# A new fixed order of all events in a delta-rule attention with a feed-forward layer

## The chip, the cores and the metric

One core of a Trainium2 chip runs the whole kernel in one launch. The metric is the device time of one execution in microseconds (us). The core has five engines that run their own instruction streams and wait for each other by semaphores: TensorE (PE, matrix products; PEld is its weight load), VectorE (DVE), ScalarE (ACT), GpSimd (POOL) and SyncE (SP), which here issues all transfers (DMA).

## The reference

What is computed, cut to what matters:

```python
# q, k, v: (4, 8, 768, 48), beta: (4, 8, 768), float32
k_n = k / (norm(k, axis=-1) + 1e-06)
state = zeros((B, H, D, D))
for t in range(S):
    y[:, :, t] = einsum('bhd,bhde->bhe', q[:, :, t], state)
    v_old = einsum('bhde,bhd->bhe', state, k_n[:, :, t])
    state = state + beta_t * einsum('bhd,bhe->bhde', k_n[:, :, t], v[:, :, t] - v_old)
x = y.transpose(0, 2, 1, 3).reshape(3072, 384)
h = x @ w_in                                   # w_in (384, 2048), float64
sp = maximum(h, 0) + log1p(exp(-abs(h)))
out = (h * erf(sp)) @ w_out                    # w_out (2048, 384), float64
```

## The kernel before, in words

The attention is cut into 12 chunks c of 64 time steps, with the 32 pairs of batch and head side by side. Per chunk: the squares of k (norm_sq, ACT L196), their sums (norm_sum, DVE L204), the norms and the factors gn and ga in 18 small steps (norm_ops, DVE L215 to L228), the products of k with itself (gram_mm, PE L255) and their scaling to the matrix A (gram_a, DVE L265). Two chunks make a group sg. A goes to DRAM (to_dram, L290) and comes back in 32x32 blocks (to_blocks, L299, tile gb). A triangular solve with 31 rows (solve_row, L316 a product, L318 an addition) inverts these blocks in tile xb; DVE does the first solve, POOL the other five. The result goes through DRAM again (put_blocks L323, from_blocks and from_blocks2 L330 and L338), is transposed (merge_t, DVE L345), and put together on PE (merge_e L353, merge_z L366, merge_m L379). Then the chain, 48 steps j (4 batches for each chunk): put_v (POOL L401, z from v and the norms), chain_u (PE L414, DVE L420), chain_s (L427), chain_y (L441), chain_m.

The outputs y are the rows x of the feed-forward layer, in 12 groups of 16 blocks: ffn1 (L631, nine products of fp16 halves), softplus and erf (ACT L653 and L658, DVE L662 and L671, ACT L669, POOL L675), ffn2 (L686 to L688), all with high and low fp16 parts. Both weights come as 24 raw pieces of 512 KB (tiles raw_in0 to 11 and raw_out0 to 11: w_load, SP L486) and pass a conversion to fp32: w_mask (ACT L493), w_sign (DVE L497), w_bits (DVE L502), w_sum (ACT L507, a copy of the absolute values that gives the maximum). The raw tiles share buffers with other tiles, so a load may wait for the w_sum of an earlier piece. When all 12 pieces of w_in are through: w_max, w_all, w_scale (DVE L511, PE L476, DVE L519), the scaled identity w_idsc (L549), the high parts w_hi (ACT L541) and the low parts (w_lo1, PE L557 and L558; w_lo2, ACT). x needs a scale as well (x_max L577, x_scale L584, x_lo L619).

At the start ACT clears xm and z by copies of a zero tile (clear_x, L164 and L166); POOL clears qp and xb. PE runs 15 zero products (warm, L153) and 270 more, one by one as events (fill), which only keep it busy.

All these steps are events with a time from a planner's formulas. The list is sorted by that time, and then put in another order by a tuple of 2554 numbers, ORDER (line 33 of the file): each engine executes its instructions in that order. This tuple alone decides what stands behind what on an engine:

```python
ev.sort(key=lambda e: (e[0], e[1]))
if ORDER:
    ev = [ev[i] for i in ORDER]
with tc.manual_schedule(engines={E.PE, E.Activation, E.DVE, E.Pool, E.SP}):
    for _, _, fn in ev:
        fn()
```

ACT loads a table of functions (table, L138) wherever the next event needs another one than the last.

## Time and profile before

| what | value |
|---|---|
| runs | 660.6, 660.2, 662.53 us (median 660.6) |
| profiled execution | 664.21 us |
| its span | 662.4 us, so 1.8 us lie around it |
| granted clock of PE, mean | 0.98 |
| busy, share of the span | PE 97%, PEld 75%, ACT 74%, DVE 63%, POOL 47% |
| zero products on PE (L153) | 285, 52.6 us |
| table loads on ACT (L138) | 147, 188.6 us |

A row of a timeline gives the start, the length, the engine, the line, the operation, out<-in with shapes, how many alike in a row (x2), and in brackets how long the engine sat idle before it and what ended that. A row of a window gives the stretch and its length, the busy time of each engine in the order PE, PEld, DVE, ACT, POOL with the number of instructions, then the granted clock, DMA's share and GB/s. L12 is line 12 of the kernel. One execution stands behind the profile; its own time is 3.6 us above the median of the runs.

### The profile page before, as it was taken

To read this page: it belongs to the slowest core of one execution; us is meant where nothing else is said; L and a number is where in the kernel's file an instruction comes from. 1 tells how busy PE (TensorE), PEld (TensorE's weight loads), DVE (VectorE), ACT (ScalarE), POOL (GpSimd) and SP (SyncE) were. 2 spreads that over 40 slices of the span, in tenths; PEclk is the share of its full clock that TensorE was granted. 3 is DMA by queue.
4 is the path that set the end of the run, shared out by engine and by line. 5 is a ranking of instruction groups with operands and counts; after the bars stand their busy time and mean duration, and the time that the engine had idled before them with its cause. 6 is when DMAs were issued, how large, how long until landed. Compare 5 with 4: busy or idle time off the path is not lost.

```text
span 662.4 us, 21898 instructions
## 1 busy us (share of the span) xinstructions
PE 639.5 (97%) x9353; PEld 493.6 (75%) x9353; DVE 415.7 (63%) x976; ACT 491.2 (74%) x731; POOL 309.5 (47%) x492
## 2 busy tenths in 40 slices
PE   7978899899999999999999999999999999999996
PEld 5655586677788878778877788887787888777763
DVE  4986877976565966677766766767454666344230
ACT  6423369899988788978678567878768879698870
POOL 2000238837588708984169274424981412403130
PEclk9979769999999999999999999999999999999999
DMA  9879763035423371423527034123014201010110
GB/s 297 250 226 280 180 160 84 30 84 106 81 68 80 90 158 38 116 48 81 119 70 174 7 99 108 32 51 74 14 25 100 64 9 44 2 25 13 25 25 24
DMA packets 87395, 59.03 MB, mean 89 GB/s; under 512 B 67777, under 2 KB 77121, under 8 KB 87297
## 3 DMA queue, kind: packets, MB, share of 16 engines
q1 hardware_dynamic: 87296, 57.63, 35.2%
q8 instruction: 73, 1.20, 0.8%
q14 instruction: 26, 0.20, 0.1%
HBM read 43.45 MB, written 14.16 MB: 87 GB/s over the span
## 4 chain that ended last, share of the span: by engine, by line
PE 73%; DVE 10%; ACT 7%; DMA 4%; POOL 2%; issue 2%; SPq 1%; DVEq 0%; POOLq 0%; ACTq 0%
PE ph L631 24%; PE pr L686 9%; PE pr L687 8%; PE pr L688 8%; PE pc L441 3%; PE pc L414 3%; DMA raw_out<-w_out 3%; PE pm L379 3%; PE pg L255 2%; PE pq L255 2%; PE pc L427 2%; PE pz L366 2%; ACT L138 2%; PE pe L353 2%; ACT w_out L541 1%
## 5 line engine op out<-in xcount | busy, mean ns | idle before, releaser
L631 PE MATMUL ph<-xh,w_in 128*128 128x256 f16 x1152 | 206.7, 273 | 0.0
L138 ACT ACT_TABLE_LOAD x147 | 188.6, 1283 | 3.3 <-PEq L959 0.7
L631 PEld LDWEIGHTS <-w_in 128*128 128x128 f16 x1728 | 166.1, 98 | 28.1 <-issue 0.9
L631 PE MATMUL ph<-xl,w_in 128*128 128x256 f16 x576 | 157.1, 273 | 0.0
L675 POOL TENSOR_TENSOR H<-L,H 128x512 f16<-128x512 f32 x58 | 69.5, 1209 | 175.6 <-DVE H L671 122.9
L662 DVE SCALAR_TENSOR_TENSOR L<-ph,L 128x512 f32<-128x512 f32 x96 | 65.8, 688 | 102.2 <-ACT L L658 93.9
L686 PE MATMUL pr<-w_out,H 128*128 128x384 f16 x384 | 125.6, 327 | 0.0
L687 PE MATMUL pr<-w_out,H 128*128 128x384 f16 x384 | 125.3, 326 | 0.2 <-DVE w_out L568 0.2
L688 PE MATMUL pr<-w_out,H 128*128 128x384 f16 x384 | 125.3, 326 | 0.0
L401 POOL TENSOR_TENSOR z<-v,nm 64x192 f32<-64x192 f32 x96 | 53.2, 555 | 132.7 <-DMA v<-vtok 111.0
L653 ACT ACTIVATE L<-ph,xct 128x512 f32<-128x512 f32 x96 | 65.9, 687 | 58.3 <-PE ph L631 51.2
L318 POOL TENSOR_TENSOR xb<-xb,tmptmpg 128x31 f32<-128x31 f32 (+15 forms) x155 | 86.6, 559 | 12.1
L316 POOL TENSOR_TENSOR tmptmpg<-gb,xb 128x31 f32<-128x31 f32 (+15 forms) x155 | 80.7, 521 | 13.0 <-DMA be<-btok 3.2
L658 ACT ACTIVATE L<-L 128x512 f32<-128x512 f32 x96 | 59.3, 628 | 0.9
L688 PEld LDWEIGHTS <-H 128*128 128x128 f16 x384 | 37.5, 98 | 25.2 <-issue 0.4
L153 PE MATMUL warm<-zero 128*128 128x384 f16 x285 | 52.6, 347 | 1.1 <-DVE zero L144 1.1
L686 PEld LDWEIGHTS <-H 128*128 128x128 f16 x384 | 37.5, 98 | 20.7
L420 DVE TENSOR_TENSOR z<-pc,ga 64x192 f32<-64x192 f32 x88 | 31.2, 354 | 34.1 <-PE pc L414 32.2
L687 PEld LDWEIGHTS <-H 128*128 128x128 f16 x384 | 37.6, 98 | 19.8
L153 PEld LDWEIGHTS <-zero 128*128 128x128 f16 x285 | 28.7, 103 | 21.9 <-issue 4.7
L255 PE MATMUL pg<-kpg 48*64 48x64 f32 x736 | 28.0, 230 | 8.3 <-DVE qp L276 4.7
L669 ACT CAST H<-L 128x512 f16<-128x512 f32 x56 | 33.5, 609 | 2.5 <-DVE L L662 2.2
(139 smaller groups left out, 929.1 us busy)
## 6 DMA issues: line engine op xcount, KB each, us to landing
raw_in<-w_in SPq DMA_DIRECT2D x12, 512.0 KB, 5.8
raw_out<-w_out SPq DMA_DIRECT2D x12, 512.0 KB, 8.7
d<-A SPq DMA_DIRECT2D x22, 256.0 KB, 3.3
kpg<-kT SPq DMA_DIRECT2D x24, 192.0 KB, 4.7
k<-ktok SPq DMA_DIRECT2D x12, 384.0 KB, 4.2
qp<-qT SPq DMA_DIRECT2D x24, 192.0 KB, 3.9
v<-vtok SPq DMA_DIRECT2D x48, 96.0 KB, 2.8
out<-ob SPq DMA_DIRECT2D x48, 96.0 KB, 2.3
```

The lines of the kernel that those rows point to most:

```text
L138: se.add_instruction(mybir.InstLoadActFuncSet(name=nc.get_next_instruction_name(), act_func_set_id=i, ins=[], outs=[]))
L153: te.matmul(wp[0], zero[:, :P], zero, start=True, stop=True)
L316: eng.tensor_tensor(tv, G[:, s, s + 1:].unsqueeze(1).broadcast_to([P, ncol, nr]), Xv[:, :, s:s + 1].broadcast_to([P, ncol, nr]), op=ALU.mult)
L318: eng.tensor_tensor(Xv[:, :, s + 1:], Xv[:, :, s + 1:], tv, op=ALU.add)
L631: te.matmul(ph, w[:, i, kt * P:kt * P + P], G[x][:, :, ksl], start=(m == 0), stop=(m == 8))
L653: se.activation(unit(g, u), G["ph", u], AF.Softplus, bias=0.0, scale=G["ct"])
L658: se.activation(Lu, Lu, AF.Erf, bias=0.0, scale=1.0)
L662: ve.scalar_tensor_tensor(Lu, fg[g]["ph", u], HSC, Lu, op0=ALU.mult, op1=ALU.mult)
L675: (ve if u % (2 if g < GLE else GLM) == 0 else ge).tensor_tensor(G["gl", u], unit(g, u), G["gh", u], op=ALU.subtract)
L686: te.matmul(G["po"][a], gh[:, o, asl], wout_h[:, i, :], start=(i == 0), stop=False)
L687: te.matmul(G["po"][a], gh[:, o, asl], wout_l[:, i, :], start=False, stop=False)
L688: te.matmul(G["po"][a], gl[:, o, asl], wout_h[:, i, :], start=False, stop=(i == NFF - 1))
```

## The change

Nothing but the tuple ORDER differs. Its first numbers, before and after:

```diff
-ORDER = (0,1,2,12,7,21,22,24,25,28,30,34,36,37,40,42,44,45,49,51,33,27,3,5,6,98,4,244,143,8,251,100,17, ...
+ORDER = (1,2,409,374,53,49,191,95,197,137,401,415,238,5,108,45,173,432,373,269,3,222,437,213,257,64,279, ...
```

The same events in another order make nearly the same instructions: the same products, transfers and vector operations; ACT loads a table 142 times in place of 147, one of them in front of the first square (line L196). The order differs over the whole list, most in the opening.

The first place is DVE in the first solve. tmpT0_n is the product of row n, w_in_100 and w_out_101 are the tiles of the converted weights. Before, a part of the solve with its pieces:

```order
L316 TENSOR_TENSOR tmpT0_5_384<-gb0_333,xb0_135 128x156
L318 TENSOR_TENSOR xb0_135<-xb0_135,tmpT0_5_384 128x6x26
L497 TENSOR_SCALAR raw_in5_364<-raw_in5_364 128x512
L316 TENSOR_TENSOR tmpT0_6_388<-gb0_333,xb0_135 128x175
L318 TENSOR_TENSOR xb0_135<-xb0_135,tmpT0_6_388 128x7x25
L497 TENSOR_SCALAR raw_in0_391<-raw_in0_391 128x512
L316 TENSOR_TENSOR tmpT0_7_557<-gb0_333,xb0_135 128x192
L318 TENSOR_TENSOR xb0_135<-xb0_135,tmpT0_7_557 128x8x24
L497 TENSOR_SCALAR raw_out3_393<-raw_out3_393 128x512
```

Now the same rows, and the place where the first piece stands:

```order
L316 TENSOR_TENSOR tmpT0_5_530<-gb0_414,xb0_379 128x156
L318 TENSOR_TENSOR xb0_379<-xb0_379,tmpT0_5_530 128x6x26
L316 TENSOR_TENSOR tmpT0_6_533<-gb0_414,xb0_379 128x175
L318 TENSOR_TENSOR xb0_379<-xb0_379,tmpT0_6_533 128x7x25
L316 TENSOR_TENSOR tmpT0_7_536<-gb0_414,xb0_379 128x192
L318 TENSOR_TENSOR xb0_379<-xb0_379,tmpT0_7_536 128x8x24
```

```order
L316 TENSOR_TENSOR tmpT0_14_558<-gb0_414,xb0_379 128x255
L318 TENSOR_TENSOR xb0_379<-xb0_379,tmpT0_14_558 128x15x17
L497 TENSOR_SCALAR raw_out1_442<-raw_out1_442 128x512
L316 TENSOR_TENSOR tmpT0_15_576<-gb0_414,xb0_379 128x256
L318 TENSOR_TENSOR xb0_379<-xb0_379,tmpT0_15_576 128x16x16
```

Rows 0 to 14 have no piece between them any more. In the whole solve there were 11 w_sign and 5 w_bits (raw_in5, in0, out3, out1, in7 first); now there are 6 w_sign (out1, out3, in9, out10, in5, in6), 3 w_bits (out10, out1, out3) and the negative identity (L546). Ahead of the solve stand seven of each before and now; the rest moved behind it.

The second place is ACT at the very start. Before:

```order
L138 ACT_TABLE_LOAD
L164 CAST xm0_0_90<-zero_102 128x1024
L164 CAST xm0_1_91<-zero_102 128x1024
L164 CAST xm1_0_92<-zero_102 128x1024
L164 CAST xm1_1_93<-zero_102 128x1024
L166 CAST z0_94<-zero_102 128x384
L166 CAST z1_95<-zero_102 128x384
```

Now:

```order
L196 ACT_TABLE_LOAD
L196 ACTIVATE sq0_172<-k0_170 128x768
L196 ACTIVATE sq1_177<-k1_145 128x768
L164 CAST xm0_0_90<-zero_102 128x1024
L164 CAST xm0_1_91<-zero_102 128x1024
L164 CAST xm1_0_92<-zero_102 128x1024
L164 CAST xm1_1_93<-zero_102 128x1024
```

The squares of chunks 0 and 1 moved ahead of the ten copies of zeros; the squares of chunks 2 and 3 stand behind them, as all four did. On DVE the sums of squares 2 and 3 now stand between the norms and the factor gn0 of the first group.

The third place is the queue of SP around the end of the first solve (d2 is the result in DRAM, A2_0 and w_out_101 blocks of A from DRAM, xm the blocks of the result). Before:

```order
L486 DMA raw_out6_758<-w_out 128x1024
L394 DMA v2_774<-vtok 128x192
L245 DMA kpq2_780<-kT 48x1024 x2
L486 DMA raw_out4_790<-w_out 128x1024
L323 DMA d2_0_792<-xb0_135 64x1024
L323 DMA d2_1_796<-xb0_135 64x1024
L330 DMA w_out_101<-d1_1_323 32x16x32 x2
L394 DMA v1_891<-vtok 128x192
L338 DMA xm0_0_90<-d2_0_792 32x16x32
```

Now:

```order
L245 DMA kpg3_763<-kT 48x1024 x2
L486 DMA raw_in11_775<-w_in 128x1024
L486 DMA raw_out6_794<-w_out 128x1024
L323 DMA d2_0_796<-xb0_379 64x1024
L330 DMA A2_0_798<-d1_0_403 32x16x32 x2
L394 DMA v0_835<-vtok 128x192
L323 DMA d2_1_840<-xb0_379 64x1024
L338 DMA xm0_0_90<-d2_0_796 32x16x32
L338 DMA xm0_1_91<-d2_0_796 32x16x32
```

The loads of raw_out4 and raw_out5 moved behind the solve's way through DRAM, two small transfers now stand between the two halves of the result, and w_out's block transfer went ahead to the first round trip. At the start of this queue k1 and k0 are now first, where kpg0 was; kpg0 is sixth.

Elsewhere: the 270 zero products, in 8 runs before (14, 133, 7, 21, 69, 18, 5, 3), stand in 21 runs (55, 1, 3, 103, 12, 5, 2, 33, 15 and twelve of 1 to 9), all ahead of the first ffn1 as before. On POOL the put_v steps 7 and 9 moved ahead of the second solve's first row, and put_v(6) behind its row 7. In the middle of the list chain steps, merges and ffn groups changed places: between the last row of POOL's last solve (sg 5) and its first merge (chunk 10) stood twelve ffn groups, and now stand five, with more chain steps.

More of the change, by code (lines that the diff above doesn't have):

```diff
@@ new lines @@
+ORDER = (1,2,409,374,53,49,191,95,197,137,401,415,238,5,108,45,173,432,373,269,3,222,437,213,257,64,279,355,112,97,225,202,169,58,4,17,18,149,19,358,20,6,26,31,307,336,247,104,35,38,399,264,420,61,27,294,390,281,98,229,304,80,255,331,43,444,129,143,7,433,153,348,100,101,8,106,235,182,338,103,47,206,155,33,164,408,178,193,46,312,21,72,76,83,60,354,146,501,521,148,15,267,528,410,162,379,421,25,389,351,286,244,11,292,234,260,317,157,302,295,428,132,12,446,87,13,387,429,251,533,549,41,440,280,330,344,175,357,123,48,135,81,366,92,337,316,78,160,99,334,52,159,102,134,67,188,385,119,89,183,284,158,296,56,242,324,272,340,270,187,210,384,425,320,118,199,113,165,107,125,342,42,32,184,16,323,150,339,392,411,84,383,190,192,195,413,328,39,365,127,171,117,419,189,62,154,82,246,258,311,211,218,70,378,91,293,376,249,196,314,181,221,347,30,224,65,219,259,86,131,233,240,248,256,262,268,276,285,291,300,308,322,315,305,74,231,28,398,198,382,289,306,217,109,168,124,326,236,1301,369,205,71,327,121,431,156,290,111,36,142,274,287,489,261,176,161,447,418,352,241,152,377,88,367,394,204,436,757,93,9,303,282,350,333,141,479,319,203,341,349,435,208,215,298,506,473,512,275,301,449,170,40,130,73,207,356,517,14,416,363,313,239,179,535,68,370,375,273,201,404,174,10,122,140,51,24,310,57,69,318,50,381,386,361,391,216,362,332,212,180,237,400,359,396,63,299,230,343,288,405,402,209,128,214,407,422,412,417,452,423,232,329,110,194,393,23,29,22,151,335,450,474,480,514,85,228,223,252,271,406,79,424,263,126,442,309,55,66,243,77,475,120,345,522,75,427,755,441,138,266,200,434,380,430,486,453,438,115,177,360,34,226,388,54,44,325,116,186,483,166,526,534,136,90,283,94,403,459,114,364,297,145,172,462,245,448,139,461,460,265,468,353,470,439,144,481,372,516,414,471,464,133,463,485,482,346,467,503,488,537,642,609,466,395,37,484,59,167,487,371,472,147,477,507,495,465,497,476,253,491,632,524,527,494,518,445,492,163,532,493,508,496,443,523,455,511,531,96,451,541,278,185,540,538,490,454,456,499,469,551,785,498,818,580,866,513,457,546,458,545,636,519,502,500,515,554,505,530,520,561,550,644,547,662,510,536,525,552,504,321,666,560,105,478,509,555,564,559,567,574,575,589,569,553,625,576,583,562,586,558,581,250,594,597,565,557,590,660,277,587,670,601,602,604,572,611,615,624,578,614,593,227,598,220,397,529,791,577,608,618,620,426,588,626,368,568,634,596,683,543,765,542,254,585,629,556,591,539,592,548,792,633,649,616,647,631,621,595,599,652,637,655,795,796,657,798,603,606,639,573,544,600,610,659,679,635,579,640,566,645,563,584,664,671,605,800,776,607,623,643,682,690,692,685,794,613,630,687,571,693,706,646,674,648,570,612,678,651,680,582,686,619,694,638,672,691,699,676,710,698,705,716,681,726,696,654,622,627,628,684,688,728,807,731,656,689,661,658,701,653,709,663,733,713,717,667,764,870,720,702,704,707,736,695,708,697,723,737,772,801,641,738,814,668,802,805,711,806,703,752,673,808,847,700,712,675,729,714,756,735,665,715,812,819,775,718,782,821,742,677,778,747,841,848,719,779,751,769,777,788,721,783,797,740,780,781,784,722,826,836,758,744,988,761,724,725,766,852,827,787,786,669,771,820,773,803,910,727,774,743,730,835,748,789,804,732,859,811,824,825,790,902,842,861,734,793,885,879,829,851,739,810,854,822,833,809,741,745,860,823,869,813,878,746,749,817,750,945,864,895,816,830,828,839,753,754,799,880,832,907,1022,831,990,867,858,617,837,872,877,838,862,871,882,853,874,834,759,857,843,887,845,849,855,840,650,916,760,929,850,873,856,922,1068,888,904,863,762,876,881,892,901,905,884,912,921,906,931,926,865,890,909,889,908,868,911,914,919,886,936,935,939,915,942,763,875,932,893,899,937,946,767,898,883,913,943,930,920,1111,897,947,844,894,925,933,1033,973,957,918,952,891,846,768,903,770,924,989,896,917,966,975,1035,934,938,951,950,962,961,941,1001,959,992,1004,995,1009,958,900,998,1279,1002,964,977,1011,963,983,1010,1053,1003,953,1012,968,1016,1034,981,1047,967,940,948,956,960,969,982,980,954,986,997,1021,971,994,1018,1000,1036,1173,1023,1052,1015,1040,1024,1037,1041,1008,991,1054,979,923,1007,1013,1058,1062,955,1116,984,993,1005,1014,1020,996,944,1064,949,927,928,1057,1061,1199,999,1006,1134,1185,1123,1192,0,1118,1066,1194,1127,1027,970,1017,1209,1028,1029,1213,1025,1032,1051,1049,1042,1043,1128,965,1131,1138,1071,1038,1141,1044,1060,976,1210,1142,1139,1031,1087,1162,987,1065,1046,1059,1083,1086,1045,978,1144,1110,1048,1055,1026,1050,1067,1056,1063,1074,1082,1075,1204,1113,1088,1146,985,1099,1085,1106,1168,1175,1147,1156,1070,1077,1232,1093,1039,1069,1019,1098,1073,815,1079,1072,1239,1096,1109,1121,1030,1129,1158,1176,1178,1182,1180,1102,1219,1076,1080,1112,1126,1186,1094,1119,1133,1078,1104,1084,1103,1140,1270,1091,1090,1148,1089,1151,1248,1097,1152,1108,1184,1115,1100,1105,1117,1092,1313,1132,1201,1159,1136,1135,1143,1150,1164,1095,1122,1149,1206,1120,1124,972,1217,1225,1172,1177,1187,1154,1189,1114,1157,1207,1238,1153,1101,1188,1107,1125,1130,1137,1145,1190,1155,1163,1227,1245,1249,1174,1160,1167,1161,1241,1171,1179,1254,1214,1263,1216,1181,1191,1381,1183,1195,1170,1246,1251,1285,1327,1373,1196,1193,1264,1265,1291,1302,1289,1284,1200,1286,1234,1306,1414,1198,1269,1255,1197,1205,1240,1299,1242,1423,1211,1215,1267,1308,1314,1229,1226,1305,1247,1262,1212,1271,1250,1257,1253,1273,1203,1208,1272,1220,1275,1223,1231,1277,1230,1237,1309,1233,1202,1350,1338,1342,1280,1228,1236,1281,1292,1244,1260,1268,1274,1282,1295,1324,1288,1341,1434,1278,1319,1332,1312,1336,1165,1235,1326,1328,1290,1330,1218,1329,1335,1222,1400,1221,1346,1360,1304,1365,1243,1375,1340,1256,1287,1224,1347,1266,1293,1389,1343,1331,1321,1334,1345,1355,1390,1349,1294,1586,1166,1169,1356,1358,1457,1276,1252,1392,1351,1303,1399,1311,1551,1310,1362,1259,1283,1348,1354,1377,1383,1387,1396,1298,1406,1408,1296,1391,1378,1384,1339,1398,1407,1333,1418,1440,1394,1344,1409,1393,1395,1425,1364,1432,1447,1419,1307,1258,1436,1261,1426,1442,1451,1413,1369,1315,1412,1359,1361,1363,1422,1367,1372,1424,1370,1430,1438,1415,1374,1371,1382,1617,1441,1366,1325,1435,1443,1453,1376,1385,1471,1337,1473,1479,1488,1428,1466,1497,1297,1460,1468,1300,1316,1352,1318,974,1491,1421,1397,1386,1402,1427,1403,1450,1357,1411,1404,1469,1323,1322,1461,1521,1416,1433,1472,1437,1525,1579,1465,1353,1464,1476,1439,1530,1539,1540,1493,1455,1417,1511,1429,1452,1480,1474,1490,1475,1484,1478,1456,1379,1499,1458,1462,1081,1485,1556,1508,1510,1368,1560,1380,1388,1401,1496,1482,1503,1512,1517,1449,1317,1515,1514,1518,1523,1524,1548,1553,1594,1446,1448,1531,1459,1467,1410,1519,1527,1481,1445,1420,1431,1444,1489,1554,1674,1561,1529,1320,1533,1494,1495,1563,1504,1454,1564,1405,1572,1546,1646,1463,1522,1558,1507,1506,1574,1565,1626,1477,1487,1498,1632,1636,1697,1528,1595,1581,1660,1470,1513,1526,1648,1587,1569,1589,1562,1532,1541,1545,1573,1483,1492,1538,1578,1486,1720,1543,1680,1571,1655,1597,1592,1557,1609,1596,1576,1535,1600,1547,1593,1580,1620,1601,1610,1624,1661,1625,1634,1598,1614,1612,1672,1640,1582,1702,1544,1638,1552,1559,1568,1649,1722,1770,1618,1652,1685,1639,1611,1536,1616,1631,1653,1659,1689,1633,1602,1566,1650,1657,1585,1604,1570,1744,1605,1666,1804,1516,1622,1588,1619,1679,1627,1658,1577,1584,1591,1607,1500,1509,1520,1534,1542,1656,1549,1688,1501,1550,1673,1555,1567,1675,1575,1628,1635,1583,1703,1705,1683,1537,1706,1690,1692,1693,1677,1728,1637,1676,1641,1707,1682,1694,1712,1724,1730,1734,1590,1740,1603,1813,1708,1710,1714,1717,1718,1844,1613,1623,1630,1643,1751,1687,1695,1654,1738,1608,1615,1761,1621,1629,1642,1651,1668,1698,1741,1736,1739,1758,1755,1662,1763,1665,1599,1502,1505,1669,1742,1670,1789,1760,1798,1606,1764,1800,1743,1759,1780,1681,1696,1786,1709,1725,1746,1731,1664,1747,1933,1745,1667,1898,1819,1762,1823,1713,1723,1767,1754,1765,2073,1753,1756,1645,1700,1671,1729,1818,1732,1701,1704,1837,1820,1779,1840,1846,1802,1805,1809,1686,1843,1771,1691,1807,1815,1783,1816,1822,1684,1699,1772,1825,1826,1835,1748,1766,1773,1838,1715,2220,1782,1781,1868,1716,1711,1964,1777,1797,1647,1872,1721,1790,1799,1808,1644,1851,1811,1719,1727,1864,1803,1812,1784,1785,1829,1726,1866,1821,1788,1879,1793,1827,1737,1787,1794,1769,1855,1735,1857,1828,1926,1878,1832,1859,1871,1862,1904,1750,1913,1752,1861,1874,1865,1870,1858,1749,1757,1877,1768,1778,1795,1886,1836,1893,1663,1876,1775,1880,1850,1932,1888,1903,1678,1911,1883,1919,1907,1791,1842,1853,1935,1841,1830,1854,1948,1957,1940,1945,1869,1905,1942,1921,1875,1959,1909,1792,1801,1920,1887,1978,1980,1884,1988,1733,1774,1776,1939,1966,1796,1892,1974,1806,1975,1925,1890,1894,1923,1961,1833,1979,1927,1983,2058,1946,1982,1984,1997,1941,1958,2000,1912,1985,1994,1998,1956,1943,1963,1929,1973,1895,1814,1824,1834,1845,1860,1965,1873,2028,2032,1885,1891,1899,1906,1917,1969,1881,1900,2004,2085,2005,1901,1924,1908,1896,1810,1817,1953,2036,2045,1931,1910,1831,1938,1967,2015,2017,1971,2054,2059,2019,2021,1839,2031,2048,1972,2061,2003,1847,2020,2067,1856,2064,1992,1949,1990,2063,2066,1981,2069,1954,1962,2018,2052,1968,1867,1849,1928,1882,1889,1934,2010,2025,1897,1902,1936,2101,2130,2023,2030,1915,1986,1944,1947,1987,2171,2202,2037,1976,2158,1914,1952,1995,2040,2001,2070,2092,1989,1996,2122,1993,2002,1922,2078,2029,2009,2106,2026,2081,2034,2047,2099,2012,2024,2050,2013,1930,2039,2046,2053,2113,2055,2060,2051,2071,1937,1848,1951,2103,2014,2088,2038,2095,2056,2135,2100,2105,2033,1852,2035,2065,1960,1970,2207,2108,2097,2079,2087,1955,2109,2094,2116,1916,2104,2107,1918,2124,2043,2044,2118,2131,2132,2120,2139,2093,2068,2154,2083,1950,2138,2102,2231,2041,2117,2080,2151,2115,2084,2134,2136,1977,2159,1991,2086,2168,2123,2126,2112,2140,2314,2072,2114,2089,2170,2157,2125,2128,2164,2121,2129,1999,2006,2141,2149,2152,2180,2172,2174,2016,2027,2176,2173,2178,2076,2077,2183,2185,2042,2074,2184,2212,2190,2187,2137,2110,2188,2244,2049,2196,2198,2142,2144,2192,2008,2143,2211,2057,2062,2177,2204,2189,2182,2208,2075,2082,2090,2011,2191,2150,2155,2209,2091,2156,2214,2219,2147,1863,2148,2163,2237,2265,2249,2096,2218,2181,2166,2245,2225,2186,2098,2256,2215,2111,2213,2217,2194,2200,2167,2243,2227,2242,2216,2226,2230,2197,2251,2259,2201,2246,2233,2261,2258,2277,2007,2203,2205,2223,2279,2119,2127,2133,2248,2238,2240,2146,2278,2263,2229,2282,2287,2247,2195,2297,2348,2221,2267,2232,2274,2266,2368,2302,2234,2273,2311,2145,2153,2250,2268,2284,2292,2160,2275,2281,2169,2272,2269,2301,2313,2179,2294,2260,2271,2300,2252,2295,2280,2323,2326,2264,2285,2286,2288,2193,2315,2199,2327,2316,2332,2317,2318,2320,2283,2255,2206,2331,2162,2022,2325,2345,2339,2210,2340,2349,2222,2350,2293,2299,2334,2298,2306,2236,2165,2352,2224,2354,2355,2357,2324,2228,2359,2333,2309,2383,2389,2175,2390,2335,2290,2235,2358,2291,2239,2373,2310,2360,2401,2362,2343,2363,2364,2241,2403,2393,2365,2254,2329,2377,2307,2319,2379,2342,2353,2344,2402,2378,2253,2381,2440,2448,2321,2328,2161,2330,2337,2449,2262,2270,2370,2356,2374,2276,2257,2338,2405,2375,2380,2392,2382,2416,2367,2417,2289,2296,2394,2456,2407,2346,2369,2457,2396,2423,2371,2425,2421,2426,2427,2303,2413,2414,2428,2431,2430,2432,2384,2387,2312,2434,2436,2322,2437,2388,2441,2336,2341,2438,2439,2347,2395,2398,2351,2361,2435,2366,2304,2443,2399,2460,2466,2442,2444,2385,2404,2406,2467,2372,2408,2429,2376,2386,2474,2475,2478,2484,2485,2492,2493,2479,2451,2453,2391,2397,2400,2410,2454,2480,2458,2409,2305,2446,2447,2459,2461,2415,2418,2496,2502,2487,2424,2433,2411,2412,2503,2308,2514,2515,2489,2445,2490,2450,2508,2494,2464,2495,2452,2511,2455,2512,2516,2463,2519,2517,2468,2469,2471,2472,2470,2420,2473,2481,2462,2518,2524,2497,2465,2525,2500,2476,2477,2532,2482,2486,2488,2491,2498,2483,2501,2499,2527,2533,2422,2419,2520,2504,2536,2538,2505,2529,2530,2507,2506,2534,2535,2539,2509,2540,2522,2523,2510,2513,2521,2526,2528,2531,2537,2541,2542,2543,2544,2545,2546,2547,2548,2549,2550,2552,2551,2553)
```

1 line of the change is left out of this document (removed).

## The prediction

> **What bounds the kernel now.** I read the page's first parts, then a table of windows, then TensorE's (PE's) and VectorE's (DVE's) timelines of the opening, backwards from the first useful matrix product. First the page: busy times, DMA's share in 40 slices of 16.6 us (tenths), the chain that ended last, and the group of the zero products.
>
> ```profile
> PE 639.5 (97%) x9353; PEld 493.6 (75%) x9353; DVE 415.7 (63%) x976; ACT 491.2 (74%) x731; POOL 309.5 (47%) x492
> DMA  9879763035423371423527034123014201010110
> PE 73%; DVE 10%; ACT 7%; DMA 4%; POOL 2%; issue 2%; SPq 1%; DVEq 0%; POOLq 0%; ACTq 0%
> L153 PE MATMUL warm<-zero 128*128 128x384 f16 x285 | 52.6, 347 | 1.1 <-DVE zero L144 1.1
> ```
>
> PE is busy 97% of the span, but 52.6 us of that are products of zeros (L153), all in the first 100 us. The chain is 73% PE and 27% other things; the other things must lie in the opening and the tail. The windows (stretch, length, busy time of each engine, granted clock, DMA share) say so.
>
> ```profile
> 100.00:200.00 100.00, 95.78 (x1501) 73.37 (x1501) 70.10 (x158) 92.14 (x158) 73.78 (x114) 1.00 0.34 75
> 200.00:640.00 440.00, 439.74 (x6545) 348.93 (x6544) 267.95 (x620) 348.69 (x476) 216.64 (x344) 1.00 0.27 62
> 640.00:662.40 22.40, 17.19 (x109) 10.42 (x107) 2.90 (x7) 5.04 (x6) 2.31 (x2) 0.94 0.14 35
> ```
>
> From 200 to 640 PE is idle 0.26 us in 440, at full clock; from 100 to 200 it is idle 4.2 us, and the tail has 5.2, a drain that stays. So the time is: the moment at which the useful stream starts, plus a fixed amount of PE work, plus a tail. A us by which the opening is shorter is a us of the end, unless a later wait takes it. The change issues the same products in both, so the fixed part stays.
>
> The stream starts with the first ffn1 product (L631) at 111.19 and is preceded by the w_lo1 products (L557), which need the scale of w_in; before that PE waits once for DVE.
>
> ```profile
> 68.57 3.35 PE L255 MATMUL pg<-kpg 48*64 48x64 f32 x64 [4.67 <-DVE qp L276]
> 111.19 0.27 PE L631 MATMUL ph<-xh,w_in 128*128 128x256 f16 x1
> ```
>
> DVE is what sets that date. It does the first triangular solve (L316, L318, 31 rows) and, between the rows, pieces of the weight conversion (w_sign L497, w_bits L502).
>
> ```profile
> 30.58 0.19 DVE L316 TENSOR_TENSOR tmpT<-gb,xb 128x31 f32<-128x31 f32 x1
> ...
> 58.36 0.43 DVE L497 TENSOR_SCALAR raw_in<-raw_in 128x512 int32<-128x512 int32 x1 [4.75 <-DMA raw_in<-w_in]
> 58.70 0.35 DVE L316 TENSOR_TENSOR tmpT<-gb,xb 128x192 f32<-128x192 f32 x1
> ...
> 65.50 0.68 DVE L502 SCALAR_TENSOR_TENSOR w_in<-w_in,raw_in 128x512 int32<-128x512 int32 x1
> 66.10 0.51 DVE L316 TENSOR_TENSOR tmpT<-gb,xb 128x31 f32<-128x31 f32 x1
> 66.64 0.21 DVE L318 TENSOR_TENSOR xb<-xb,tmpT 128x31 f32<-128x31 f32 x1
> ...
> 74.23 1.43 DVE L345 STREAM_TRANSPOSE T<-xm 32x512 f32<-32x512 f32 x2 [1.32 <-DMA xm<-d]
> ...
> 99.02 0.40 DVE L549 TENSOR_SCALAR ids_in<-ident,sc_in 128x128 f32<-128x128 f32 x1
> ```
>
> The solve runs from 30.58 to 66.85, 36.27 us. In it stand 7.1 us of waits for weight loads, by the list of DVE's waits in this stretch (in total, times, longest):
>
> ```profile
> DVE raw_in L497 <- DMA raw_in<-w_in: 4.8, 1, 4.8
> DVE raw_out L497 <- DMA raw_out<-w_out: 2.3, 2, 1.2
> ```
>
> A row that needs nothing from the weights stands behind a w_sign whose load is late. The longest goes back to the load queue, which SyncE (SP) issues in order: between these two rows SP stood for 9.6 us at a load whose buffer was still in use.
>
> ```profile
> 33.32 1.60 SPq L188 DMA_DIRECT2D qp<-qT  x2
> 44.54 0.35 SPq L486 DMA_DIRECT2D raw_in<-w_in  x1
> ```
>
> **The change part by part.** No instruction of PE, DVE, POOL or SP is added or removed in kind; what moves is the order, and five table loads of ScalarE (ACT) go (147 become 142).
>
> *Squares first.* ACT now squares k0 and k1 ahead of clearing xm and z; in the trace they stood behind.
>
> ```profile
> 2.02 3.88 ACT L164 CAST xm<-zero 128x1024 f32<-128x1024 f16 x4
> 5.82 2.57 ACT L166 CAST z<-zero 128x384 f32<-128x384 f16 x6
> 8.29 2.31 ACT L196 ACTIVATE sq<-k 128x768 f32<-128x768 f32 x3
> ```
>
> ```profile
> k<-ktok SPq DMA_DIRECT2D x12, 384.0 KB, 4.2
> ```
>
> ```profile
> 16.98 1.29 DVE L265 TENSOR_TENSOR A<-pg,gn 128x512 f32<-128x512 f32 x2
> ```
>
> k1 and k0 are now first in SP's queue, so the two squares end near 6.9 (issue near 1.2, 4.2 to land, 0.77 each). DVE's first norm can then start 3 us earlier than behind the clearing. But the scale gn0 stands behind the sums of the two other squares, and those behind the 6.45 us of clearing: 6.9 + 6.45 + 1.54 = 14.9 for the last square, 0.9 for its sum, about 0.2 for each of six small steps (like the first rows of the solve): 17.0. To that comes kpg0, whose load was first in the queue and is now sixth. So the first product with gn0 comes between 17 and 18.5, where it came at 17.0; behind it the two round trips through DRAM, and as many weight pieces ahead of the solve as before (seven of each kind). I take +1.8 us for the start of the solve, with bounds 0 and +2.5. It cannot gain much, since as many pieces fill DVE until then.
>
> *Pieces out of the solve.* Before, 11 w_sign and 5 w_bits stood between rows; now 6 and 3, and none before row 15, plus one small cast of the identity. A w_sign takes 0.34 of the train of instructions (58.36 to 58.70), a w_bits 0.60 (65.50 to 66.10). So 5 x 0.34 + 2 x 0.60 = 2.9 us less, 0.13 more for the cast. By my walk through the new list (an estimate from these durations), the loads of the pieces left land 8 us or more ahead of their w_sign, since SP now issues most of them just behind the first DRAM round trip and none stands in the first 15 rows; a load lands 5.8 us (raw_in) or 8.7 us (raw_out) after its issue, in the median. The 7.1 us of waits go too. Together -9.8; bounds -2.8 (all waits stay) and -10.
>
> ```profile
> raw_in<-w_in SPq DMA_DIRECT2D x12, 512.0 KB, 5.8
> raw_out<-w_out SPq DMA_DIRECT2D x12, 512.0 KB, 8.7
> ```
>
> *From the solve to the transposes.* 66.85 to 74.23 before, with DMA the last to come (1.32). Now put_blocks(0) and its way back are no longer behind put_blocks(1), but a v load stands between. I take -0.7, bounds 0 and -1.3.
>
> *From the transposes to the w_in scale.* 74.23 to 99.02 is merges, chain steps and the rest of the pieces on DVE. The pieces taken out of the solve are not free: 7 of them (2.9 us) have to be done somewhere. Where they stood before the w_in maximum they push it back; but w_out pieces now stand behind it, and DVE waits here for PE in two places. I take -1.5, bounds +3 and -2.5.
>
> *Loads of v on POOL, zero products, table loads.* POOL's second solve should start with the chain steps that feed it, some us earlier; work that was not late for PE is worth nothing by itself. The zero products keep their number; they are cut in 21 runs instead of 8. At idle time they cost nothing; their cost is the clock (rival A). Five table loads fewer are ACT time in the steady part, where PE is not waiting for ACT: nothing.
>
> *What the path cannot show.* Each moved step now hands over somewhere else. After 100 us the largest single waits of PE on such handovers are those before its x products:
>
> ```profile
> PE sp L476 <- DVE xm L577: 1.8, 2, 1.6
> ```
>
> I allow +1.7 for one of that kind. Sum: +1.8 - 9.8 - 0.7 - 1.5 + 1.7 = -8.5. Checked by the far end: the first ffn1 would come near 102.7, and all of it reaches the end only if no wait follows. The profiled execution took 664.21 (span 662.4 and 1.8 around it); the sum makes it 655.7. The median of the runs is 660.6, 3.6 less; against it the time is 652.
>
> **Rivals.**
>
> *A, slower: the clock.* PE's clock fell to half three times in the opening; the fourth row is the w_lo1 stage.
>
> ```profile
> 38.40:45.30 6.90, 5.65 (x57) 3.94 (x59) 6.49 (x16) 3.07 (x7) 1.07 (x2) 0.51 0.46 121
> 69.20:76.00 6.80, 6.80 (x64) 4.47 (x60) 5.42 (x10) 2.49 (x6) 1.00 (x2) 0.50 0.68 134
> 82.80:93.10 10.30, 9.58 (x204) 9.03 (x202) 8.72 (x17) 5.58 (x17) 3.10 (x6) 0.50 0.73 179
> 99.40:111.20 11.80, 11.47 (x116) 6.91 (x114) 9.31 (x30) 10.53 (x25) 10.38 (x20) 1.00 0.49 114
> ```
>
> The second follows the idle 4.67 us of PE. The zero products are what kept PE busy; spread out in 21 runs, they may leave PE idle in more places, so that it enters the w_lo1 stage at half clock. That stage's 11.47 us of products would take up to 22, and the chain steps ahead of them some 4 longer: -8.5 + 10.5 + 4 = +6, 666. It decides if half clock lasts past about 100. Against it: the fourth row has full clock although PE had been at half for 10 us shortly before (third row), and the stage itself is dense. The Trainium skill ("TensorE: Matmul & The Clock Gate", "What's actually happening") says that the throttled state is the default and activity releases it, by a window of about 3.4 us. The trace agrees with half clock after an idle of 4.67 us; by that rule thinner zero products speak against this change, and the time would be this rival's, not the forecast's. Chance 0.07.
>
> *B, given back later.* In the fifth POOL solve, the new list leaves only five ffn groups on PE between its last row and its merge, where twelve stood; a group is about 1 us (9 products 0.11 apart, from the pitch of L631, or 6 of ffn2), chain steps add some 2.8: 7.7 us. Before, that distance was
>
> ```profile
> 493.70 0.27 POOL L318 TENSOR_TENSOR xb<-xb,tmptmpg 128x31 f32<-128x31 f32 x1
> ...
> 508.81 1.20 PE L353 MATMUL pe<-T,A 32*32 32x32 f32 x64
> ```
>
> about 14.8 us, and in the opening the way through DRAM alone took 7.4 (66.85 to 74.23) and the transposes 1.43. If POOL's last row is as late against PE as there, PE waits 2 to 7 us; 4 would make 656. Against: the list also lets POOL begin that solve with more PE work ahead. Chance 0.16.
>
> *C, it doesn't do what it says: the loads are still late.* The page's DMA line stands at 7 to 9 tenths in the first five slices, and the same bytes must come. If the six pieces left in the solve wait as long as before, 7.1 come back: 659. For it: SP still has loads that wait for a buffer ahead of put_blocks. Against: the rows before 15 have no piece at all in them. Chance 0.12.
>
> **How the numbers follow.** The forecast has 0.62, more gain than forecast (the transposes stage at its -2.5, and a start without delay: 647) 0.03. The range goes from 646.5 (-14, all terms at their good ends) to 658.5, which leaves out C's upper half and A, under 0.15. The forecast's own range is 648.5 to 655.5. A measurement tells 0.5%, 3.3 us, from no change: 657.3 to 663.9 is the same. Faster: forecast, B and the extra gain, and a little of C: 0.82; same: most of C and a bad B, 0.11; slower: A, 0.07.
>
> **What would show it.** DVE in the solve: no wait of L497 longer than 0.3, the rows ending near 59, transposes near 66.5; the diagonal of the w_in scale (L549) 89 to 91, first ffn1 102 to 105, PE idle from 200 on under 1 us. Wrong if L497 still waits for DMA (C), if the granted clock is half in the w_lo1 stage (A), or if PE has a wait of several us before L353 near 500 (B).

## The result and the profile after

Over 20 executions each the new order takes 657.28 us in the median (652.96 to 662.8) and the order before 662.02 (659.1 to 663.88): ratio 0.9933, 95% interval 0.991 to 0.9956, which is 4.4 us faster (the medians differ by 4.7). One execution of the new order (662.8) counts as slow and is left out of the ratio and of the table of clocks below. The forecast was 8.5 us faster, 652. The direction was right and the size about twice what came: 657.28 lies inside the whole range of 646.5 to 658.5, but outside the forecast's own 648.5 to 655.5.

The two profiled executions alone differ by what was forecast, 664.21 before and 655.81 after, 8.4 us. That is luck: the one before is longer than the median of its kernel, the one after shorter than 16 of the other 24 of its own. The parts of the page of the new order:

```profile
PE 635.8 (97%) x9353; PEld 488.7 (75%) x9353; DVE 423.6 (65%) x976; ACT 484.2 (74%) x726; POOL 313.8 (48%) x492
DMA  8996872337231451534461036611131101000020
PE 79%; DVE 8%; ACT 5%; POOL 3%; issue 2%; DMA 1%; SPq 1%; POOLq 0%; DVEq 0%
L153 PE MATMUL warm<-zero 128*128 128x384 f16 x285 | 54.2, 345 | 1.1 <-DVE zero L144 1.1
```

Idle time of PE is span less busy time: 662.4 - 639.5 = 22.9 before, 654.0 - 635.8 = 18.2 after, 4.7 less. The other 3.7 us of the 8.4 are busy time, of the same products; the clock of the two executions differs (mean 0.98 and 0.99), which would do that. The windows (columns as before) from 100 us on:

```profile
100.00:200.00 100.00, 98.32 (x1560) 76.42 (x1559) 74.11 (x160) 95.00 (x163) 79.72 (x119) 1.00 0.35 78
200.00:640.00 440.00, 439.79 (x6513) 347.55 (x6514) 268.56 (x606) 337.92 (x461) 212.95 (x332) 1.00 0.27 60
640.00:654.00 14.00, 8.78 (x55) 5.09 (x52) 0.62 (x1) 0.58 (x1) 0.00 (x0) 0.89 0.12 28
```

From 200 to 640 PE is idle 0.21 us, and 1.7 from 100 to 200 where it was 4.2: nothing was given back in the steady part, and 2.5 us were won just ahead of it. The milestones of DVE in the profiled execution, by its timeline (start, length, line):

```profile
19.16 1.29 DVE L265 TENSOR_TENSOR A<-pg,gn 128x512 f32<-128x512 f32 x2 [1.75 <-PE pg L255]
...
34.47 0.18 DVE L316 TENSOR_TENSOR tmpT<-gb,xb 128x31 f32<-128x31 f32 x1
...
61.05 0.21 DVE L318 TENSOR_TENSOR xb<-xb,tmpT 128x31 f32<-128x31 f32 x1
...
67.67 1.42 DVE L345 STREAM_TRANSPOSE T<-xm 32x512 f32<-32x512 f32 x2
...
91.88 0.58 DVE L549 TENSOR_SCALAR ids_in<-ident,sc_in 128x128 f32<-128x128 f32 x1
```

The first ffn1 product, with which the prediction let the useful stream start, came 3.3 us earlier than the 111.19 of before:

```profile
107.89 0.27 PE L631 MATMUL ph<-xh,w_in 128*128 128x256 f16 x1
```

From the scale of w_in to this product it is 16.0 us where it was 12.2. PE waits 0.3 us in them; more products stand ahead of it, among them ten zero products in place of three. So the date of this product can't be compared between the two orders, and the scale of w_in is the better mark.

DVE's only wait between 30 and 62 us is this one, ahead of the solve; inside the solve no piece waits for a load:

```profile
DVE w_in L502 <- DVE raw_in L497: 0.5, 1, 0.5
```

### The profile page after: what moved, and what is told of

The parts are those of the page before. It is cut to its first block, busy times and chain, and to the rows that moved or that the text cites. A ratio compares the mean times of both kernels' runs of the same rounds, so it can differ in the third digit from the quotient of the medians.

```text
span 654.0 us, 21873 instructions
## 1 busy us (share of the span) xinstructions
PE 635.8 (97%) x9353; PEld 488.7 (75%) x9353; DVE 423.6 (65%) x976; ACT 484.2 (74%) x726; POOL 313.8 (48%) x492
## 4 chain that ended last, share of the span: by engine, by line
PE 79%; DVE 8%; ACT 5%; POOL 3%; issue 2%; DMA 1%; SPq 1%; POOLq 0%; DVEq 0%
PE ph L631 26%; PE pr L686 9%; PE pr L688 9%; PE pr L687 9%; PE pc L441 3%; PE pc L414 3%; PE pm L379 3%; PE warm L153 3%; PE pg L255 2%; PE pq L255 2%; PE pc L427 2%; PE pz L366 2%; PE pe L353 2%; DVE xb L318 2%; DVE tmpT L316 2%
## 5 line engine op out<-in xcount | busy, mean ns | idle before, releaser
L316 POOL TENSOR_TENSOR tmptmpg<-gb,xb 128x31 f32<-128x31 f32 (+15 forms) x155 | 82.5, 532 | 29.7 <-DMA A<-d 12.5
L318 POOL TENSOR_TENSOR xb<-xb,tmptmpg 128x31 f32<-128x31 f32 (+15 forms) x155 | 88.8, 573 | 12.1
L153 PE MATMUL warm<-zero 128*128 128x384 f16 x285 | 54.2, 345 | 1.1 <-DVE zero L144 1.1
L420 DVE TENSOR_TENSOR z<-pc,ga 64x192 f32<-64x192 f32 x88 | 31.3, 355 | 30.4 <-PE pc L414 23.2
L675 DVE TENSOR_TENSOR H<-L,H 128x512 f16<-128x512 f32 x38 | 33.1, 877 | 2.5 <-ACT H L669 2.3
```

The source lines that it names most:

```text
L153: te.matmul(wp[0], zero[:, :P], zero, start=True, stop=True)
L316: eng.tensor_tensor(tv, G[:, s, s + 1:].unsqueeze(1).broadcast_to([P, ncol, nr]), Xv[:, :, s:s + 1].broadcast_to([P, ncol, nr]), op=ALU.mult)
L318: eng.tensor_tensor(Xv[:, :, s + 1:], Xv[:, :, s + 1:], tv, op=ALU.add)
L675: (ve if u % (2 if g < GLE else GLM) == 0 else ge).tensor_tensor(G["gl", u], unit(g, u), G["gh", u], op=ALU.subtract)
```

## The experiments

Theory 1 in the expectations: the order is worth more than 4 us, and half clock on useful products in a part of the executions takes some back. Theory 2: the clock does not matter. In the diffs a name is an event of the list, and fill one zero product. The runs were taken in four series on four chips; each ratio is to the order before in its own series (medians 660.75, 660.91, 661.74 and 662.02 us).

**The new order again, with the clock of each execution.** No edit.

> The new order unchanged, as the yardstick for the other kernels on the same chip. Both theories: about 0.993 of the order before (median near 657), with executions from 653 to 662. Theory 1 (clock): the executions with the lower mean clock are the longer ones, about 0.45 us longer for each us at half clock, so 7 us between a mean clock of 0.992 and one of 0.977. Theory 2 (transfers or waits differ from run to run, not the clock): time and mean clock are not ordered together.

Measured: 657.18 us, ratio 0.9932 (0.9905 to 0.9958). The executions differ by their clock. Of the timed executions of the two kernels whose clock is on record (25 of the new order; 72 of the order before, from the four series), the mean time by mean clock:

| mean clock of the execution | before: us (executions) | after: us (executions) |
|---|---|---|
| 0.99 and more | 658.9 (2) | 654.5 (6) |
| 0.985 to 0.99 | 660.4 (17) | 656.2 (8) |
| 0.98 to 0.985 | 661.3 (33) | 659.1 (8) |
| under 0.98 | 662.4 (20) | 660.3 (3) |

A line through the single executions gives 0.35 us for each us at half clock in the new order (0.45 was expected; correlation 0.85) and 0.18 in the order before (0.58). This does not say how much of it the clock causes: long waits of PE lengthen an execution and may lower its clock as well. The profiled execution here is of a lower clock (span 656.6) than the one above (654.0). The chain stage of both, in a window of each (from DVE's first chain step, L420, to the scale of w_in, roughly):

```profile
77.40:92.50 15.10, 13.20 (x330) 11.40 (x330) 11.69 (x32) 10.04 (x25) 2.96 (x6) 0.89 0.74 199
78.00:94.50 16.50, 16.50 (x361) 13.91 (x357) 11.54 (x31) 9.93 (x24) 2.86 (x5) 0.70 0.66 175
```

The first window is of the first execution, at clock 0.89, the second at 0.70. The same stage took 14.5 us in one (chain step at 77.38, scale at 91.88) and 16.1 in the other (77.98, 94.04), and PE sat idle 1.9 us in the one and not at all in the other. So the execution at the lower clock is 1.6 us longer here. This is what rival A described, in another stage and at a smaller size.

**More zero products, in both orders.**

```diff
 # new order: 14 ahead of gram_mm(2,1), 20 ahead of gram_mm(3,1), 4 ahead of each of five chain steps
+fill x54
 # order before: 10, 16 and 26 ahead of three groups of gram products, 4 ahead of each of five steps
+fill x72
```

> The new order with 54 more zero products: 14 and 20 ahead of the two groups of gram products where PE sat idle 3.0 and 3.8 us, and 4 each ahead of five chain steps. Theory 1 (the half clock falls on useful products in a part of the executions): mean clock 0.99 or more in all, median 652 to 654, spread under 4 us. Theory 2 (the clock is not what decides): median 657 as without them, or 2 to 4 us later where the 20 small ones delay the chain.

> The order before with 72 more zero products in the same way: 10, 16 and 26 where PE sat idle 1.9, 2.9 and 4.7 us, 4 each ahead of five steps of the chain stage. Theory 1: the 24 us at half clock shrink to under 8, and the time falls by 2 to 5 us (the half clock of 82.8 to 93.1 lay on useful products, about 10 us of it). Theory 2: 662, no change.

Measured: 663.53 (1.0035, 1.0017 to 1.0053) and 664.3 (1.0043, 1.0017 to 1.007), both slower than the order before. The first one's profiled execution has a mean clock of 0.995, and still 660.2 of span. Its PE in the chain stage:

```profile
87.29 0.82 PE L153 MATMUL warm<-zero 128*128 128x384 f16 x4
88.04 0.56 PE L427 MATMUL pr<-z,k 64*48 64x48 f32 x16
88.53 0.67 PE L414 MATMUL pr<-z,xm 128*64 128x48 f32 x16
```

There is no idle time ahead of or behind the zero products: in this stretch PE is packed, and each one is paid in full. The scale of w_in came at 95.75 where it was 91.88. Another 2.3 us were lost behind it (566.2 us from the scale to the end, where it was 563.9), most of it as idle time of PE behind 100 us, 4.1 us where it was 1.9. What theory 1 hoped to win by the clock was more than paid for. That the order before lost as well was not expected by either theory. In its profile the zero products take 64.4 us, 10 to 12 more than in four profiles without the addition, and PE's idle time is 16.5 us, 3 to 7 less: by this, PE's idle time took in only about half of them. It also had 6.8 us of half clock at 133 to 140, but so have profiles of the order before itself (below).

**One part of the change alone: pieces out of the end of the solve.**

```diff
 # order before
-..., w_sign(in,3), ..., w_sign(in,10), ..., w_sign(in,9), w_sign(in,6), w_sign(out,6), w_bits(in,10), solve_row(0,30), ...
+..., solve_row(0,30), w_sign(in,3), w_sign(in,10), w_sign(in,9), w_sign(in,6), w_sign(out,6), w_bits(in,10), ...
 # and w_sign(out,1) just ahead of w_bits(out,1)
```

> The order before with one part of the change alone: the five w_sign from raw_in3 on (in3, in10, in9, in6, out6) and w_bits of in10 stand behind the first solve's last row, and w_sign of out1 just ahead of its w_bits. Theory 1: the 4.8 and 1.2 us of waits and 2.4 us of pieces leave the solve, its end comes near 59, and 4 to 7 us of it reach the end of the kernel (656 to 658). Rival: the pieces behind the solve, or merges that wait for PE, push the maximum of w_in back to where it was: 660 to 662.

Measured: 658.8 (0.9957, 0.9931 to 0.9983), 2.0 us faster than the 660.75 of its series, between the theory and the rival. The interval stands for 1.1 to 4.6 us, so it does not say more closely what share of the whole change this part is. The solve's last row moved by 9.2 us against the profile of before, the transposes by 3.2 (8.5 and 2.4 against the means of four profiles, below):

```profile
57.47 0.21 DVE L318 TENSOR_TENSOR xb<-xb,tmpT 128x31 f32<-128x31 f32 x1
...
62.71 0.43 DVE L497 TENSOR_SCALAR raw_out<-raw_out 128x512 int32<-128x512 int32 x1 [3.70 <-DMA raw_out<-w_out]
...
70.99 1.42 DVE L345 STREAM_TRANSPOSE T<-xm 32x512 f32<-32x512 f32 x2
```

The wait for raw_out6 only moved behind the solve (3.7 us at 62.7), and between the last row and the transposes DVE does 7 w_sign and 3 w_bits, where it did 2 and 2. Taking work and waits out of the solve pays less than it takes out, as long as the same DVE does the rest ahead of the next stage.

**A shorter way to the first A.**

```diff
 # new order
-..., clear_x, put_v(2), ..., norm_sq(2), ..., gram_mm(1,0), ..., norm_sq(3), gram_mm(0,1), ..., gram_mm(0,0), ...
+..., norm_sq(2), ..., norm_sq(3), clear_x, put_v(2), gram_mm(0,1), ..., gram_mm(0,0), gram_mm(1,0), ...
 # and 18 of the 55 first fills moved to the run inside the solve
```

> The new order with a shorter way to the first A: all four squares ahead of the clearing of xm and z (POOL's first put_v behind it), the gram products of chunk 0 ahead of those of chunk 1, and 18 of the 70 first zero products moved to the run inside the solve. In the new order gn0 came at 17.2 and the first gram_a at 19.2 (70 zero products hold PE until 15.0), 2.2 later than before. Theory (the late start of the solve took 2 us of the forecast gain): first gram_a near 14, solve from 30 to 32 in place of 34.5, 1.5 to 3 us faster than the new order (654 to 655.5 where that has 657). Rival (the opening's end is set by DVE's work after the solve, the w_in pieces): solve earlier, end within 1 us of the new order.

Measured: 657.36 (0.9948, 0.9922 to 0.9974), no gain over the new order. The first A came 4.2 us earlier, at 15.0, but the solve only from 34.47 to 34.0:

```profile
15.01 1.28 DVE L265 TENSOR_TENSOR A<-pg,gn 128x512 f32<-128x512 f32 x2
...
21.76 0.69 DVE L502 SCALAR_TENSOR_TENSOR w_in<-w_in,raw_in 128x512 int32<-128x512 int32 x1 [4.19 <-ACT w_in L493]
```

The clearing, now behind the squares, holds back ACT's w_mask, and DVE waits 4.2 us for it with the second half of A queued behind. The expectation had left out what stands behind clear_x on ACT. The time is the rival's, but the early solve that the rival granted did not come either.

**Zero products taken from the late part, and all of them.**

```diff
 # new order, 10 late ones
-w_max(in), ..., fill x10 among x_tr and w_lo1
+fill x10 ahead of gram_mm(0,0,pq), in the solve
 # new order, all 61 behind the solve
-put_blocks(0), ..., fill x61
+fill x61 ahead of gram_mm(0,0,pq)
 # new order, and order before, without any
-fill x270
```

> The new order with the last 10 zero products, those behind the w_in maximum (among the w_lo1 products), moved to the run inside the solve. Theory (in this stage PE is never idle, so zero products stand on the path at their full 0.16 us): 1.6 us faster than the new order. Rival (they keep the clock up): half clock in the w_lo1 stage, 2 to 6 us slower.

> The new order with all 61 zero products behind put_blocks(0) moved to the run inside the solve. Theory (path): the 30 or so behind the first transposes go, 2 to 4 us faster than the new order at equal clock; the 20 that stood in PE's idle time gave nothing. Rival (clock): the wait of PE at 62 to 67 leaves the chain stage at half clock in most executions, mean clock 0.975, and the gain is eaten: 0 to 3 us slower than the new order.

> The new order without the 270 zero products (15 at the start stay). It prices rival A of the prediction: if the zero products keep the clock open, half clock spreads over most of the opening (60 us or more) and the time grows by 5 to 15 us; if PE's clock follows the useful products alone, the time is that of the new order or 2 us less.

> The order before without the 270 zero products. Beside the new order without them (655.7) it gives the gain of the new order with zero products out of the account and the clock at half until late in both. Theory 1 (the order of loads, pieces and norms is worth 5 to 6 us, and zero products that stand on the path take 2 of it back): 660.5 to 662, as with them, since there nearly all stand in PE's idle time. Theory 2 (the order is worth 4 us and the zero products cost both the same): 658.5 to 659.5.

Measured: 10 late ones moved, 654.42 (0.99, 0.9869 to 0.993); all 61 moved, 657.46 (0.9938, 0.9916 to 0.996); none in the new order, 655.66 (0.9907, 0.9876 to 0.9938); none in the order before, 660.33 (0.998, 0.996 to 0.9999).

For the 10 late ones 1.6 us less than the new order were expected, and 2.8 came (654.42 against 657.18), but not for the theory's reason. In the w_lo1 stage the 10 products cost little: from the first w_lo1 to the first ffn1 it is 14.6 us (92.50 to 107.12) without them and 14.8 (93.13 to 107.89) with them. What differs is the clock: 5 of its 6 executions have 0.99 or more, against 6 of 25 of the new order, and at that clock both take the same (654.6 and 654.5). The moved products fill a part of PE's waits near 43 us (3.2 idle in two waits before, 2.2 now); that this raised the clock is not shown by six executions. With all 61 moved, the clock is under 0.98 in all 8 executions, at half from 63 to 91 in the profiled one, and the time is 657.5, as the rival (clock) had it:

```profile
63.30:90.50 27.20, 20.85 (x488) 19.35 (x484) 21.82 (x42) 11.41 (x29) 2.01 (x4) 0.50 0.82 201
```

Without any zero products PE is at half clock for some 72 us, until 88, and the kernel is no slower (655.66; the intervals overlap, so that it is faster is not shown). Rival A's price of 14 us for such a case was far too high, since full clock comes back before the w_lo1 stage. What the kernel wins is at the start: the 70 first zero products hold PE until 15.0, the first A comes at 19.16 with them (row above) and at 17.44 without, the solve at 34.47 and 32.55. The scale of w_in comes at 91.95, as in the first profile with them (91.88): the way from the solve to there took back what the start won.

```profile
1.12 13.90 PE L153 MATMUL warm<-zero 128*128 128x384 f16 x70 [1.12 <-DVE zero L144]
```

Without zero products the new order is 4.7 us faster than the old one (660.33 to 655.66), about as with them, and 4.8 us by the two ratios, each to its own series: the rest of the order is worth 4 to 5 us without its zero products. Which parts of it, only the run with the pieces moved tells, and for one part.

**Zero products moved at both ends.**

```diff
 # new order
-fill x55, gram_mm(1,0), fill, gram_mm(0,1), fill x3, gram_mm(0,0), gram_mm(1,1), ..., w_max(in), ..., fill x10
+fill x37, gram_mm(1,0), gram_mm(0,1), gram_mm(0,0), gram_mm(1,1), ..., fill x32, gram_mm(0,0,pq), ..., w_max(in), ...
```

> The new order with 32 zero products moved to the run inside the solve: 22 of those ahead of the last of the first gram products, and the 10 behind the w_in maximum; nothing else. Without any zero products the first gram_a came at 17.4 in place of 19.2 and the solve at 32.6 in place of 34.5. Theory (those zero products stood on the path at both ends): solve from about 32.6, 1.5 to 2 us faster than with the late 10 alone, 4 to 5 faster than the new order: 652 to 653. Rival (only the late ones count, the start is made up for by DVE's work before the w_in maximum): 654 to 655. The best of the kernels if the theory holds.

> As the kernel with both ends moved, and six more zero products moved that stand between the first chain step and the w_in maximum. Theory (PE is packed there too): another 0.5 to 1 us faster, 651.5 to 652.5. Rival (clock): half clock through the chain stage in more executions, mean clock lower, 1 to 2 us slower than that kernel.

> The kernel with 22 zero products moved from the start and 10 from behind the w_in maximum once more, for a narrower interval and a second profile: 653 to 656 in the median, 0.987 to 0.992 of the order before.

Measured: 654.67 (0.9896, 0.9864 to 0.9929), and the same kernel again 652.9 (0.986, 0.9844 to 0.9877): 7 to 9 us below the order before. The first time fits the rival, the second the theory; the second interval lies below that of the new order (0.991 to 0.9956), the first overlaps it. The solve starts 1.5 to 2.2 us earlier than in the new order:

```profile
32.24 0.18 DVE L316 TENSOR_TENSOR tmpT<-gb,xb 128x31 f32<-128x31 f32 x1
...
90.28 0.58 DVE L549 TENSOR_SCALAR ids_in<-ident,sc_in 128x128 f32<-128x128 f32 x1
```

With six more moved out of the chain stage it is 655.17 (0.9897, 0.9879 to 0.9915), no further gain; its profiled execution has 6.8 us of half clock at 82 to 89, so the rival (clock) fits, but with so few executions it is not settled.

**Three more profiles of the order before.** No edit. What was open is how typical the execution was from which the terms were taken.

> The order before, unchanged, another look at one execution. The sum of the prediction was made on an execution 3.6 us above the median. Theory (that execution had later weight loads and more half clock on useful products than most): the waits of DVE for loads inside the first solve add up to 4.5 to 5 us in place of 7.1, the solve ends near 64.3 in place of 66.9, the first ffn1 product comes 1.5 to 3 us before 111.2. Rival (the loads are as late in every execution and the 3.6 us lie elsewhere): 6.5 to 7.5 us of waits, solve end 66 to 67.

> The same kernel, a second look, to see how far the waits inside the solve differ from one execution to the next. Theory: 4 to 6 us. Rival: 6.5 to 7.5.

> The same kernel, a third look. Theory: 4 to 6 us of waits inside the solve. Rival: 6.5 to 7.5.

Measured: 665.77, 662.17 and 661.49 us. DVE's waits for loads between 30 and 67 us, one pair of rows for each profile (in total, times, longest):

```profile
DVE raw_in L497 <- DMA raw_in<-w_in: 3.9, 1, 3.9
DVE raw_out L497 <- DMA raw_out<-w_out: 1.6, 2, 1.0
```

```profile
DVE raw_in L497 <- DMA raw_in<-w_in: 3.9, 1, 3.9
DVE raw_out L497 <- DMA raw_out<-w_out: 0.9, 1, 0.9
```

```profile
DVE raw_in L497 <- DMA raw_in<-w_in: 3.0, 1, 3.0
DVE raw_out L497 <- DMA raw_out<-w_out: 1.7, 2, 1.4
```

5.5, 4.8 and 4.7 us where the first profile had 7.1. The solve's last row came at 66.56, 64.77 and 65.86, and the scale of w_in at 98.89, 94.75 and 96.65 (99.02 in the first profile). The end of the solve in the first of the three and its 111.1 for the first ffn1 fit the rival; its waits and the other two profiles fit the theory. Its time, 665.77, is the longest of its kernel though its waits are shorter, so the waits alone do not make an execution slow. From the scale of w_in to the end it is 566.9, 567.4 and 564.8 us (565.2 in the first profile). The two longest of these four have 3.4 and 6.8 us of half clock between 129 and 138; the others have none between 100 and 200.

## Why the prediction was right or wrong

With four profiles of the order before and two of the new one, each step of the sum can be set beside means:

| step | forecast | order before, mean of 4 | new order, mean of 2 | measured |
|---|---|---|---|---|
| start of the solve | +1.8 | 31.39 | 34.30 | +2.9 |
| solve, first to last row | -9.8 | 34.57 | 26.62 | -8.0 |
| last row to transposes | -0.7 | 7.45 | 6.62 | -0.8 |
| transposes to scale of w_in | -1.5 | 23.92 | 25.43 | +1.5 |
| scale of w_in to the end (the wait allowed for) | +1.7 | 566.08 | 564.11 | -2.0 |
| sum | -8.5 | 663.41 | 657.08 | -6.3 |

The mechanism is as told in the main: the solve lost its waits and 7 of its 16 pieces, and the scale of w_in comes 4.4 us earlier. That this is also the 4.4 us by which the runs differ is chance. The executions in this table differ by 6.3 us, since 2.0 were won behind the scale, and the four of before average 663.4 where the median is 662.0. What failed is the size of four terms, and the execution against which they were taken.

- *From the transposes to the scale* is the largest shortfall, -1.5 forecast and +1.5 measured, inside its bounds of +3 and -2.5. It counted on w_out pieces passing behind the w_in maximum; the 2.9 us of the seven pieces moved out of the solve were named and not put in. In the rows of DVE 1 w_sign and 7 w_bits stood between the transposes and the scale, and now 4 and 6 do. Of the seven pieces one went ahead of the transposes, two into this stage and only four behind the scale. DVE's work in the stage did not shrink (third busy time in each row, first the profile of before, then that of the new order, up to the end of the scaling):

```profile
74.23:99.42 25.19, 23.51 (x584) 20.03 (x582) 20.57 (x44) 13.35 (x33) 8.21 (x18) 0.76 0.77 186
67.67:92.46 24.79, 22.11 (x597) 18.08 (x592) 20.99 (x47) 13.91 (x35) 4.09 (x8) 0.93 0.79 200
```

In the means it grew by 0.5 us (20.0 to 20.5, up to the start of the scaling). The other 1.0 us is idle time of DVE, which is longer where more half clock falls into the stage: in the order before 2.7, 3.5, 5.0 and 4.6 us with 2.4, 6.8, 9.0 and 12.0 us of it, in the new order 3.8 and 6.1 with 3.4 and 17.1. With two profiles of the new order its share is not settled.

- *Pieces out of the solve* was mis-sized, -9.8 forecast and -8.0 measured: the 7.1 us of waits were one execution's. The others have 4.7 to 5.5, with which the same sum gives -7.5 to -8.3. The statement that a sum made against one execution can be taken off the median failed with it: that execution lay 3.6 us above the median of three runs, 2.2 above that of 20, and a part of that was in the term itself.
- *Squares first* was mis-sized: +2.9 in the means and +3.9 between the first two profiles, outside its bounds of 0 to +2.5. The working stopped at gn0, which came at 17.2, nearly as worked out; then DVE waited 1.75 us for PE, which ran 70 zero products until 15.0 and only then the first gram products. That is the sentence "At idle time they cost nothing" failing: the ones ahead of the first gram products did not stand in idle time. Without zero products in either order the solve starts at 30.55 and 32.55, and the +2.0 is close to the forecast.
- *From the solve to the transposes* was right in size, and DVE's wait for DMA ahead of the transposes (1.1 to 1.3 us in the four profiles) is gone.
- *What the path cannot show* had the wrong sign: +1.7 was allowed for a wait, and 2.0 us were won. The first x product waits 0.3 us now where such waits took up to 1.6, and from 100 to 200 PE is idle 1.7 and 2.1 us where it was 3.4 to 4.2. About half of the 2.0 goes with the half clock at 129 to 138 in two profiles of before; against the other two the new order wins 0.9.
- Of the signs that were named, DVE's waits in the solve, PE's idle time from 200 to 640 (0.2 us, under 1) and the full clock in the w_lo1 stage came as told. The last row (61, said near 59), the transposes (67.4 and 67.7, said 66.5), the scale (91.9 and 94.0, said 89 to 91) and the first ffn1 (107.9 and 110.1, said 102 to 105) all came late. The 647 given for the extra gain does not follow from its terms, which make about 649.
- Rival A: wrong in place and size, right in kind. Half clock never reached the w_lo1 stage, but the chain stage was 1.6 us longer in the execution that had more of it, and the time goes with it by 0.35 us for each us in the new order and 0.18 in the old one; why the two differ is not shown. The rule of the Trainium skill's "TensorE: Matmul & The Clock Gate" ("What's actually happening"), that activity releases the throttled state, agrees with the kernel without zero products (mean clock 0.944 and 72 us at half in the profiled execution). What this rival drew from it, that the time must then grow, does not hold there.
- Rival B: no trace shows it; PE has no wait between 440 and 520 in either profile of the new order. Rival C: no load is waited for in the solve, so it fell.

## What to carry to other kernels

Before a wait is costed from one profile, look at several executions of the same kernel: waits for loads here differed by half their size, and a forecast from a slow execution promises its bad luck as gain. Compare the end as well as the milestone, in the same executions: two numbers that agree may be of different executions. Work moved out of a serial stretch of an engine is worth its waits, and of the work itself only what also passes behind the next thing that engine owes: here four pieces of seven. Products that only keep the clock up are not free where their engine is packed or late: count what stands directly behind each run of them, and try the kernel without.

## What the runs showed of the hardware

Half clock came in stretches of about 3.4 us or a multiple of it: 43.5 to 46.9, 64.0 to 67.4 and 84.4 to 87.8 in the new order's first profile, 6.8, 6.8 and 10.2 us in that of before, 17.1 in the second profile of the new order, 27.3 with 61 zero products moved and 78.5 in the order before without any. The one at 84.4 began 1.0 us after an idle time of PE of only 1.9 us, in the middle of small products. The one at 82.8 in the profile of before began without any such time: in the 6.8 us ahead of it PE was busy 5.98 us and waited 0.4 us at the longest.

Which stage they fall on differs from execution to execution of one kernel. Four of seven profiles of the order before and its variants have one between 129 and 140 us; in ten of the new order and its variants none lies between 91 us and the last 5 us. In the new order the mean clock goes with most of the spread of 10 us (correlation 0.85).
